# Value passes unit by unit, expert products in strips of 32 columns, and wider spacing of the score groups in an attention and expert kernel

## The chip, the cores and the metric

The kernel runs on one core of one Trainium2 chip. The metric is the device time of one execution in microseconds (us), the median of three runs; lower is better.

## The reference

```python
# q, k, v: (8 batches, 12 heads, 448 tokens, 64)
scores = (1 / sqrt(64)) * q @ k^T;  attn = softmax(scores);  a = attn @ v
x = a.transpose(0, 2, 1, 3).reshape(3584, 768)
h = x @ w_in               # 768 x 2048
g = h * sigmoid(h)
out = g @ w_out            # 2048 x 768, float32
```

## The kernel before

**Units.** Heads go in groups of four, three groups to a batch. A unit is one group of one batch: 448 queries (in batch 0, 224, so that it starts sooner). The 448 keys of a group are laid out as four chunks. The first four groups are "lone": their chunks have 128, 128, 96 and 96 keys. The others go in pairs, ten of them: each has three full chunks and a rest of 64 keys, and the rests of the two groups of a pair stand in one chunk, the "low" group's in partitions 0 to 63 and the "high" group's in 64 to 127.

**TensorE's four shapes.** A matmul may use only part of the array, and then several run at once.

- Scores (`score`, L323): 32 rows by 128 columns, the four heads at once, each over 64 channels in two steps (L327). A pair has three score groups for each unit and one for both rests (`scores_rest`, 32x64, eight matmuls at once for each step).
- Sums (`attend_sums`, L398): 128x32, four heads at once, three steps for a pair (L406).
- Value passes (`attend`, L414): one for each half of the 64 output channels (`part` 1 and 2). For a pair one pass makes both units: three steps of 128x32 for each, in two PSUM banks, then one step of eight 64x32 matmuls for the two rests (L390 through `attend_mm`). That is seven steps, 24 matmuls of 128x32 and 8 of 64x32.
- Experts: full 128x128. `ffn1` (L484) multiplies by `w_in`, six matmuls of 448 columns for each of 16 blocks (L487). `product` (L682) multiplies by `w_out` with a scheme of seven products in the place of eight for two token tiles and two column halves (a "quad", L685), eight matmuls of 384 columns each; the sums that it needs are made on VectorE (`combine_g`, L656). The first four output tiles are made plainly (`plain`, L695, L699). The last two batches' `w_in` products use a scheme of seven too (`pair_product`, L603, L622).

**Other engines.** ScalarE makes the exponentials (L364), tanh (L498) and later silu, VectorE the transposes of Q and K, the reciprocals of the sums, the scaling of the value passes (`norm`, L468, L473) and the gates (L533). GpSimd issues all loads, in the order of `plan_k`, `plan_q` and `plan_v`; SyncE issues the stores.

**The order of the work** is not that of loops. `Order` (L78) is a planner that runs while the kernel is built: each piece of work is an `Op` with an engine, a guessed time and what it depends on; the planner steps a clock, and at each step gives ScalarE and VectorE the ready `Op` that has waited longest (corrected by a bias), and TensorE what the loop at L1443 picks. The code is then emitted in the planned order, and the engines follow it by semaphores. The loop picks a score group if its inputs and buffers are ready and the planned clock has come to `pace["next"]` (or no expert work is ready), and runs ready value work behind it; otherwise ready value work if there is any; otherwise the first ready expert product of the list `moe`. `pace["next"]` goes up by `PACE` for each score group of batches from 2 on. It may lag behind the clock by a credit of 4 us. A change of shape is charged with `SWITCH` (0.094 us, `on_pe`, L106). `Ring`s stand for buffers: two pairs of PSUM banks for scores, four banks ("m") for all other outputs, nine tiles of exponentials, two tiles of V. `SHY` makes VectorE hold back unimportant work if urgent work is about to come.

Of the kernel before, what the change touches and what calls it, by code (L numbers as in the profile page):

```python
# [9 lines left out]
FP16 = mybir.dt.float16  # L10
# [54 lines left out]
class Op:  # L65


    def __init__(self, eng, busy, emit, deps=(), bias=0.0, tail=HOP, then=None):
        self.eng, self.busy, self.emit = eng, busy, emit
        self.deps, self.bias, self.tail, self.then = list(deps), bias, tail, then  # L70
        self.done = None
        self.half = False

    def ready(self):
# [3 lines left out]
class Order:  # L78


    def __init__(self, shy):
        self.now, self.shy = 0.0, shy
        self.free = {"PE": 1.0, "ACT": 2.1, "DVE": 1.2, "POOL": 1.2}
        self.wait = {"ACT": [], "DVE": []}
        self.pool = []
        self.dma_free = 0.0
        self.out = []
        self.mode = None
        self.busy = {e: 0.0 for e in self.free}

# [7 lines left out]
    def start(self, op):  # L98
        self.emit(op.emit)
        self.free[op.eng] = self.now + op.busy  # L100
        self.busy[op.eng] += op.busy
        op.done = self.now + op.busy + op.tail
        if op.then:
            op.then(op.done)

    def on_pe(self, op, mode):  # L106
# [59 lines left out]
def kernel(  # L166
# [28 lines left out]
    NRK, NRQ = 3, 4  # L195
    PACE = 2.6
    LONES = (0, 1, 2, 3)
# [4 lines left out]
    COLD, FIRST = 8.5, 47  # L202
    SHY = 0.5
    TWB, SXB = 4, 4
# [33 lines left out]

    rawk, rawq, KT, QT, VT, E, T, acc, rdn_t, xT, g_t, ost_t = ({} for _ in range(12))
    sT_t, inv_t = {}, {}  # L240
# [23 lines left out]
    def load_v(b, hg0, hg1, x):  # L264
        if b not in VT:
            VT[b] = sb.tile([128, NH, NCH, D], FP16, name=f"V_{b}", tag="V", bufs=2)
        hs = slice(HG * hg0, HG * hg1)
        first, count = X_TOK[form(b, hg0)][x]
        nc.gpsimd.dma_start(  # L269
            out=VT[b][32 * x : 32 * (x + 1), hs, 0:count, :],  # L270
            in_=v[b, hs].rearrange("h (i g) d -> i h g d", g=TPP)[
                :, :, first : first + count, :
            ],
        )
# [107 lines left out]
    def attend_mm(a, n, part, c, h, k0, k1, e, start, stop):  # L382
        b, hg, g0, g1 = units[n]
        nq = 32 * (g1 - g0)
        at = nq * (c % per_burst(n))
        if part == 0:
            w = ones[k0:k1, :]
        else:
            w = VT[b][k0:k1, HG * hg + h, c, part - 1 :: 2]
        nc.tensor.matmul(  # L390
            out=a[32 * h : 32 * (h + 1), 0:nq],
            lhsT=w,
            rhs=e[k0:k1, h, at : at + nq],
            start=start,
            stop=stop,
        )
# [17 lines left out]
    def attend(ns, part):  # L414
        made = []
        lone = len(ns) == 1
        if part == 0 and not lone:
# [66 lines left out]
    def ffn1(b, f, t0, t1):  # L484
        h = ps.tile([128, 512], FP32, name=f"h_{b}_{f}_{t0}", tag="m", bufs=4)
        for cc in range(NDC):
            nc.tensor.matmul(  # L487
                out=h[:, 0 : t1 - t0],
                lhsT=w_in_t[:, cc, 128 * f : 128 * (f + 1)],
                rhs=x3(b, cc)[:, cc % 3, t0:t1],  # L490
                start=(cc == 0),
                stop=(cc == NDC - 1),
            )
        h_t[(b, f, t0)] = h
# [60 lines left out]
    def old_buffer(name, home, cols):  # L555

        if home == "V":
            t = sb.tile([128, NH, NCH, D], FP16, name=name, tag="V", bufs=2)
            t = t.rearrange("p h c d -> p (h c d)")
# [43 lines left out]
    def pair_product(f, m):  # L603
# [17 lines left out]
        for c in range(3):  # L621
            nc.tensor.matmul(  # L622
                out=pp_t[(f, PBANK[m])],
                lhsT=w[:, c, :],
                rhs=a[:, c, :],
                start=(c == 0 and m in (1, 6, 5)),
                stop=(c == 2),
                skip_group_check=True,
            )
# [45 lines left out]
    def product(qd, m):  # L675
# [8 lines left out]
        for f in range(HF):  # L684
            nc.tensor.matmul(  # L685
                out=pr_t[(qd, BANK[m])][:, 0:OH],
                lhsT=w[:, f, :],
                rhs=W_[m][:, f, :],
                start=(f == 0 and BANK[m] == m),
                stop=(f == HF - 1),  # L690
                skip_group_check=True,
            )


    def plain(t, j, f0, f1):  # L695
        if f0 == 0:
            pr_t[("o", t, j)] = ps.tile([128, 512], FP32, name=f"o_{t}_{j}", tag="m", bufs=4)
        for f in range(f0, f1):
            nc.tensor.matmul(  # L699
                out=pr_t[("o", t, j)][:, 0:OH],  # L700
# [228 lines left out]
    def queue_pair():  # L929
        xs = {(r, c): x_op[(PB + r, c, 0)] for r in range(2) for c in range(NDC)}  # L930
        v_ring.take()
        e_ring.take(2)
        od.add(
            Op(
                "ACT",
                2.7,
                first_silu,
                [x for f in range(NFF) for x in g_op[(PB - 1, f)]],
                -5,
            )  # L940
        )
        for m in range(1, 5):
# [8 lines left out]
        for f in range(HF):  # L951
            queue_pair_f(f, xs)

    def queue_pair_f(f, xs):
# [284 lines left out]
    jobs.sort()  # L1239
    qk_seq, av_seq = [], []  # L1240
    for ns in jobs:
# [85 lines left out]
    def av_at():  # L1327
# [3 lines left out]
        if len(ns) == 2 and part == 0:  # L1331
            if any(len(t_op.get(n, ())) < 2 for n in ns):
                return None
# [6 lines left out]
        for n in ns:  # L1340
            if len(exp_op.get(n, ())) < 2 * NCH // per_burst(n):
                return None
            first = 0.0 if n == ns[0] else (NCH - 1) * mm(S)
            for i, x in enumerate(exp_op[n]):
                c = i // 2 * per_burst(n)
                if len(ns) == 2 and c == NCH - 1:
                    c = 2 * (NCH - 1) - (n != ns[0]) * (NCH - 1)
                deps.append((x, first + c * mm(32 * (units[n][3] - units[n][2]))))
            if part:
# [10 lines left out]
    def run_av():  # L1360
# [4 lines left out]
        if part == 0:  # L1365
            m_ring.take()
            mms = 3 if two else 4
        else:
            m_ring.take(len(ns))
            mms = 7 if two else 4  # L1370
        op = Op(
            "PE",
            mms * mm(nq) + 0.013 + (0.03 + SWITCH if two and part else 0.0),
            lambda: attend(ns, part),
            tail=PE_OUT,
        )
        if part == 2:

            def then(at):
                for _ in range(7 if two else NCH // per_burst(ns[0])):  # L1380
                    e_ring.give(at)
                if any(units[n][1] == NG - 1 and units[n][3] == TPP for n in ns):
                    v_ring.give(at)

            op.then = then
# [3 lines left out]
        if two and part:  # L1389
            od.mode = "rest cols"  # L1390
        if part == 0:
# [51 lines left out]
    while True:  # L1443
        plan_turns(qk_seq[0][0][0] + 3 if qk_seq else NU)
        plan_adds()
        plan_pair()
        plan_sums()
        soon = od.step()
        if od.free["PE"] <= od.now:
# [81 lines left out]
```

## Time and profile before

| | |
|---|---|
| median of 3 runs | 396.54 us (396.23 to 396.64) |
| profiled execution | 396.11 us, of which the span is 394.3 us |
| instructions | 9242 |
| granted TensorE clock | 1.0 in every slice |
| VectorE, ScalarE busy | 69%, 64% of the span |
| DMA | 34.43 MB in 35579 packets, mean 87 GB/s |

The span is the time from the first to the last instruction of the program; the rest of the execution lies around it. In rows of the time line a start, a length, the engine, the line, the operation, `out<-in`, the shape of the array (rows*columns), the shape of the moving operand and a count follow one another. Matmuls overlap in the pipeline, so a row's length is longer than the distance to the next start: the distance is what a piece of work costs.

### The profile page before, as it was taken

To read this page: it belongs to the slowest core of one execution; us is meant where nothing else is said; L and a number is where in the kernel's file an instruction comes from. 1 tells how busy PE (TensorE), PEld (TensorE's weight loads), DVE (VectorE), ACT (ScalarE), POOL (GpSimd) and SP (SyncE) were. 2 spreads that over 40 slices of the span, in tenths; PEclk is the share of its full clock that TensorE was granted. 3 is DMA by queue.
4 is the path that set the end of the run, shared out by engine and by line. 5 is a ranking of instruction groups with operands and counts; after the bars stand their busy time and mean duration, and the time that the engine had idled before them with its cause. 6 is when DMAs were issued, how large, how long until landed. Compare 5 with 4: busy or idle time off the path is not lost.

```text
span 394.3 us, 9242 instructions
## 1 busy us (share of the span) xinstructions
PE 387.6 (98%) x3679; PEld 200.0 (51%) x3679; DVE 272.7 (69%) x570; ACT 253.6 (64%) x404; POOL 83.6 (21%) x153
## 2 busy tenths in 40 slices
PE   8999999999999999999999999999999999999995
PEld 7667764443444444554444444444444555555563
DVE  2466676999967588963698576896879945457332
ACT  4988885696871986753974759867685236763221
POOL 7532547215001532330006131600000000000000
PEclk9999999999999999999999999999999999999999
DMA  7999999919033946292016683711100130001343
GB/s 116 204 210 210 162 179 187 154 35 141 13 65 79 148 56 86 50 193 62 2 23 90 116 162 52 98 24 31 51 2 7 33 99 25 2 1 29 95 110 90
DMA packets 35579, 34.43 MB, mean 87 GB/s; under 512 B 11600, under 2 KB 34000, under 8 KB 35536
## 3 DMA queue, kind: packets, MB, share of 16 engines
q0 software_dynamic: 24784, 22.82, 38.7%
q1 hardware_dynamic: 9984, 10.24, 9.6%
q10 hardware_dynamic: 768, 0.79, 0.8%
q8 instruction: 29, 0.48, 0.5%
q14 instruction: 14, 0.11, 0.1%
HBM read 45.61 MB, written 11.01 MB: 144 GB/s over the span
## 4 chain that ended last, share of the span: by engine, by line
PE 91%; DVE 4%; ACT 1%; DMA 1%; issue 1%; ACTq 0%; POOL 0%; DVEq 0%; POOLq 0%
PE p L685 28%; PE h L487 28%; PE s L327 12%; PE a L390 10%; PE f L622 8%; PE o L699 3%; PE a L406 2%; DMA rq<-in_q_dram 1%; DVE tw L598 1%; ACT E L364 1%; PE z L1438 1%; DVE G L533 1%; ACTq L734 0%; DVE S L671 0%; DVE G L671 0%
## 5 line engine op out<-in xcount | busy, mean ns | idle before, releaser
L364 ACT ACTIVATE E<-s 128x896 f16<-128x896 f32 (+1 forms) x172 | 149.9, 915 | 22.6 <-PE s L327 21.2
L487 PE MATMUL h<-xT,w_in_t 128*128 128x448 f16 (+1 forms) x672 | 118.9, 327 | 0.0
L487 PEld LDWEIGHTS <-w_in_t 128*128 128x128 f16 x672 | 61.1, 98 | 54.4 <-issue 18.8
L498 ACT ACTIVATE th<-h 128x448 f16<-128x448 f32 (+1 forms) x112 | 54.3, 495 | 31.6 <-PE h L487 21.5
L533 DVE SCALAR_TENSOR_TENSOR G<-th,h 128x448 f16<-128x448 f16 (+2 forms) x112 | 55.1, 507 | 16.0 <-ACT th L498 14.0
L685 PE MATMUL p<-w_out_t,G 128*128 128x384 f16 x368 | 65.3, 326 | 0.3 <-DVE xT L473 0.2
L685 PEld LDWEIGHTS <-G 128*128 128x128 f16 x472 | 45.3, 98 | 33.4 <-issue 4.0
L269 POOL DMA_DIRECT2D V<-in_v_dram x88 | 48.6, 570 | 57.1 <-PE a L390 43.6
L327 PE MATMUL s<-rq,KT 32*128 32x448 f16 (+4 forms) x864 | 56.7, 340 | 0.6 <-ACT E L364 0.4
L742 ACT COPY ost<-p 128x384 f32<-128x384 f32 x39 | 18.7, 479 | 48.5 <-PE p L685 33.5
L390 PE MATMUL a<-E,V 128*32 128x448 f16 (+3 forms) x864 | 40.6, 335 | 0.0
L473 DVE SCALAR_TENSOR_TENSOR xT<-a,rdn 128x448 f16<-128x448 f32 (+1 forms) x54 | 28.9, 568 | 12.5 <-PE a L390 11.7
L254 POOL DMA_DIRECT2D rq<-in_q_dram x27 | 15.2, 561 | 105.2 <-PE s L327 85.8
L685 PE MATMUL p<-D,S 128*128 128x384 f16 x208 | 37.4, 327 | 0.0
L327 PEld LDWEIGHTS <-KT 32*128 32x128 f16 (+2 forms) x864 | 17.5, 98 | 28.7 <-issue 25.9
L390 PEld LDWEIGHTS <-V 128*32 128x32 f16 (+2 forms) x864 | 18.2, 95 | 22.6 <-issue 15.3
L375 DVE TENSOR_TENSOR T<-T,E 128x1792 f16<-128x1792 f16 x20 | 21.7, 1086 | 11.4 <-ACT E L364 11.4
L685 PEld LDWEIGHTS <-S 128*128 128x128 f16 x208 | 19.4, 98 | 16.2 <-issue 3.1
L375 DVE TENSOR_TENSOR T<-E,E 128x1792 f16<-128x1792 f16 x20 | 21.7, 1083 | 7.8 <-ACT E L364 7.8
L647 ACT ACTIVATE G<-f 128x448 f16<-128x448 f32 x32 | 16.2, 547 | 8.4 <-PE f L622 8.3
L304 DVE STREAM_TRANSPOSE KT<-rk 128x256 f32<-128x256 f32 (+3 forms) x48 | 16.6, 384 | 5.9 <-DMA rk<-in_k_dram 5.8
L314 DVE STREAM_TRANSPOSE rq<-rq 128x448 f32<-128x448 f32 (+1 forms) x27 | 15.3, 570 | 6.0 <-DMA rq<-in_q_dram 5.9
(124 smaller groups left out, 323.6 us busy)
## 6 DMA issues: line engine op xcount, KB each, us to landing
out_dram<-ost SPq DMA_DIRECT2D x208, 48.0 KB, 1.6
rk<-in_k_dram POOLq DMA_DIRECT2D x24, 224.0 KB, 4.9
rq<-in_q_dram POOLq DMA_DIRECT2D x21, 224.0 KB, 5.2
w_in_t<-in_moe_w_in_dram POOLq DMA_DIRECT2D x6, 512.0 KB, 11.6
w_out_t<-in_moe_w_out_dram POOLq DMA_DIRECT2D x4, 768.0 KB, 12.9
V<-in_v_dram POOLq DMA_DIRECT2D x43, 64.0 KB, 3.8
V<-in_v_dram POOLq DMA_DIRECT2D x40, 48.0 KB, 3.6
out_dram<-ost ACTq DMA_DIRECT2D x16, 48.0 KB, 1.8
```

The costliest lines, as they stand in the source:

```text
L269: nc.gpsimd.dma_start(out=VT[b][32 * x : 32 * (x + 1), hs, 0:count, :], in_=v[b, hs].rearrange("h (i g) d -> i h g d", g=TPP)[:, :, first ...
L327: nc.tensor.matmul(out=pS[p0 : p0 + 32 * (x1 - x0), h % 2, at : at + nq], lhsT=KT[(b, hg)][32 * h : 32 * (h + 1), c, x0:x1, :, e], rhs=QT[ ...
L364: nc.scalar.activation(out=E[(n, w)][0:kr, 2 * y : 2 * y + 2, 0:nk], in_=pS_t[(n, w, y)][0:kr, :, 0:nk], func=AF.Exp, scale=attn_scale,)
L375: nc.vector.tensor_tensor(out=T[n], in0=T[n] if step else E[(n, 0)], in1=E[(n, step + 1)], op=ALU.add,)
L390: nc.tensor.matmul(out=a[32 * h : 32 * (h + 1), 0:nq], lhsT=w, rhs=e[k0:k1, h, at : at + nq], start=start, stop=stop,)
L473: nc.vector.scalar_tensor_tensor(out=x3(b, cc)[:, cc % 3, 32 * g0 : 32 * g1], in0=acc[(n, part)][:, 0:nq], scalar=0.5, in1=rdn_t[n].rearra ...
L487: nc.tensor.matmul(out=h[:, 0 : t1 - t0], lhsT=w_in_t[:, cc, 128 * f : 128 * (f + 1)], rhs=x3(b, cc)[:, cc % 3, t0:t1], start=(cc == 0), s ...
L498: nc.scalar.activation(out=th, in_=h_t[(b, f, t0)][:, 0 : t1 - t0], func=AF.Tanh)
L533: nc.vector.scalar_tensor_tensor(out=dst[:, f, at + lo : at + hi], in0=th_t[(b, f, t0)][:, lo - t0 : hi - t0], scalar=1.0, in1=h_t[(b, f, ...
L622: nc.tensor.matmul(out=pp_t[(f, PBANK[m])], lhsT=w[:, c, :], rhs=a[:, c, :], start=(c == 0 and m in (1, 6, 5)), stop=(c == 2), skip_group_ ...
L685: nc.tensor.matmul(out=pr_t[(qd, BANK[m])][:, 0:OH], lhsT=w[:, f, :], rhs=W_[m][:, f, :], start=(f == 0 and BANK[m] == m), stop=(f == HF - 1),
L742: nc.scalar.copy(out=ost(qd, i, j), in_=bank(qd, m))
```

## The change

1. **Value passes unit by unit.** `av_seq` has the sums of a pair as before, and then parts 1 and 2 of each unit by itself, in one PSUM bank: four steps of four 128x32 matmuls. The fourth step takes the shared chunk with all 128 rows; for the other unit's half to add nothing, V holds zeros there. The two V tiles become fixed buffers, and `clear_v` writes these zeros: two memsets at the start, four when batches 0 and 1 are done with their tiles.
2. **Experts in strips.** While attention isn't finished and the four plain tiles are planned, `ffn1`, `product` and the others run each matmul as four of 128x32, one for each 32 output rows, over the same moving operand (`wide`). The planner counts them as the shape of the value passes ("cols"), without a change.
3. **Spacing.** `PACE` goes from 2.6 to 4.0 and the credit from 4 to 8 us. `SHY` goes to 0.
4. The first silu, which loads ScalarE's table, is planned when all value passes and the last `ffn1` have been planned.

```diff
     def on_pe(self, op, mode):
+        if mode == "full" and self.attention:
+            mode, op.strips = "cols", True
         gap = SWITCH if mode != self.mode else 0.0
...
-    PACE = 2.6
+    PACE = 4.0
...
-    SHY = 0.5
+    SHY = 0.0
...
+    VT = [const.tile([128, NH, NCH, D], FP16, name=f"V{i}") for i in range(2)]
+
+    def clear_v(i, hg, low):
+        rows = slice(64, 128) if low else slice(0, 64)
+        nc.vector.memset(VT[i][rows, HG * hg : HG * (hg + 1), NCH - 1], 0.0)
+
+    for hg in (1, 2):
+        clear_v(1, hg, hg == 1)
...
+    def wide(out, lhsT, rhs, **flags):
+        n = 4 if od.strips else 1
+        for j in range(n):
+            at = slice(128 // n * j, 128 // n * (j + 1))
+            nc.tensor.matmul(out=out[at], lhsT=lhsT[:, at], rhs=rhs, **flags)
...
         for n in ns:
             a = ps.tile([128, 512], FP32, name=f"a_{n}_{part}", tag="m", bufs=4)
-            made.append(a)
             acc[(n, part)] = a
-            for c in range(NCH if lone else NCH - 1):
+            for c in range(NCH):
+                e = E[(lead.get(n, n) if c == NCH - 1 else n, c // per_burst(n))]
                 for h in range(HG):
                     attend_mm(
-                        a, n, part, c, h, 0, rows_of(n, c), E[(n, c // per_burst(n))],
-                        c == 0, lone and c == NCH - 1,
-                    )
-        if not lone:
-            for h in range(HG):
-                for i, n in enumerate(ns):
-                    attend_mm(
-                        made[i], n, part, 3, h, 64 * i, 64 * (i + 1), E[(ns[0], 3)],
-                        False, True,
+                        a, n, part, c, h, 0, rows_of(n, c), e, c == 0, c == NCH - 1
                     )
...
-            nc.tensor.matmul(
+            wide(
                 out=h[:, 0 : t1 - t0],
...
-        av_seq += [(ns, part) for part in range(3)]
+        av_seq.append((ns, 0))
+        av_seq += [([n], part) for n in ns for part in (1, 2)]
+        lead[ns[-1]] = ns[0]
...
+        od.attention = bool(qk_seq or av_seq) and len(plain_op) == 4
...
-                pace["next"] = min(max(pace["next"], od.now - 4), od.now) + (
+                pace["next"] = min(max(pace["next"], od.now - 8), od.now) + (
                     PACE if u0[0] > EAGER else 0.0
                 ) * len(qk_seq[0][2]) / 2
```

More of the change, by code (lines that the diff above doesn't have):

```diff
@@ L72, in __init__ @@
         self.half = False
+        self.strips = False
     def ready(self):
@@ L88, in __init__ @@
         self.mode = None
+        self.strips = False
+        self.attention = True
         self.busy = {e: 0.0 for e in self.free}
@@ L414, in attend @@
     def attend(ns, part):
-        made = []
-        lone = len(ns) == 1
-        if part == 0 and not lone:
+        if part == 0 and len(ns) == 2:
             attend_sums(ns)
@@ L952, in queue_pair, with plan_silu @@
             queue_pair_f(f, xs)
+    silu_op = []
+    def plan_silu():
+        if silu_op or av_seq or ffn1_left[PB - 1]:
+            return
+        deps = [x for f in range(NFF) for x in g_op[(PB - 1, f)]]
+        silu_op.append(od.add(Op("ACT", 1.4, first_silu, deps, -5)))
     def queue_pair_f(f, xs):
@@ L1239 @@
     jobs.sort()
-    qk_seq, av_seq = [], []
+    qk_seq, av_seq, lead = [], [], {}
     for ns in jobs:
@@ L1342, in av_at @@
                 return None
[L1343 removed]
             for i, x in enumerate(exp_op[n]):
                 c = i // 2 * per_burst(n)
[L1346 to L1348 removed]
+                deps.append((x, c * mm(32 * (units[n][3] - units[n][2]))))
             if part:
@@ L1368, in run_av @@
         else:
-            m_ring.take(len(ns))
-            mms = 7 if two else 4
+            m_ring.take()
+            mms = 4
         op = Op(
             "PE",
-            mms * mm(nq) + 0.013 + (0.03 + SWITCH if two and part else 0.0),
+            mms * mm(nq) + 0.013,
             lambda: attend(ns, part),
@@ L1379, in then @@
             def then(at):
-                for _ in range(7 if two else NCH // per_burst(ns[0])):
+                n = ns[0]
+                for _ in range(NCH // per_burst(n) - (lead.get(n + 1) == n)):
                     e_ring.give(at)
@@ L1383, in then @@
                     v_ring.give(at)
+                    i = units[ns[-1]][0]
+                    for hg in range(NG if i == 0 else 1 if i == 1 else 0):
+                        low = i == 0 and hg != 1
+                        od.add(
+                            Op("DVE", 0.2, lambda hg=hg, low=low: clear_v(i, hg, low), [op], 5)
+                        )
             op.then = then
```

36 lines of the change are left out of this document (13 added, 23 removed).

## The prediction

> **What bounds the kernel now.** I read the engine sums first, then TensorE's waits, then TensorE's time line.
>
> ```profile
> PE 387.6 (98%) x3679; PEld 200.0 (51%) x3679; DVE 272.7 (69%) x570; ACT 253.6 (64%) x404; POOL 83.6 (21%) x153
> ```
>
> ```profile
> PE a L390 <- issue: 0.5, 1, 0.5
> ```
>
> TensorE is busy for 98% of the span, and once it has begun its longest wait is this one of half a microsecond. So the time is the sum of TensorE's own work, and the only thing to gain is what TensorE spends that isn't streaming. In the two stretches below the columns are: length, busy time and instructions of matmuls, weight loads, DVE, ACT and POOL, then clock, DMA share and GB/s:
>
> ```profile
> 14.40:27.40 13.00, 13.00 (x294) 8.34 (x293) 7.85 (x23) 11.83 (x14) 6.31 (x10) 1.00 1.13 210
> 75.60:305.30 229.70, 229.58 (x2126) 102.89 (x2123) 179.15 (x358) 161.18 (x242) 46.60 (x86) 1.00 0.41 69
> ```
>
> The second stretch is what the change works on: from the end of the four plain output tiles (75.6) to the last value pass (305.4). The groups of that stretch, by shape:
>
> ```profile
> L487 PE MATMUL h<-xT,w_in_t 128*128 128x448 f16 x480 | 98.9, 353 | 0.0
> L685 PE MATMUL p<-w_out_t,G 128*128 128x384 f16 x216 | 39.1, 326 | 0.1
> L327 PE MATMUL s<-rq,KT 32*128 32x448 f16 x408 | 29.3, 360 | 0.0
> ...
> L685 PE MATMUL p<-D,S 128*128 128x384 f16 x112 | 20.4, 327 | 0.0
> L685 PE MATMUL p<-D,G 128*128 128x384 f16 x56 | 10.3, 327 | 0.0
> L390 PE MATMUL a<-E,V 64*32 64x448 f16 x144 | 6.9, 360 | 0.0
> L327 PE MATMUL s<-rq,KT 32*64 32x448 f16 x144 | 5.4, 368 | 0.0
> ```
>
> 480+216+112+56 and 24 more of the products on X (26 with two last plain ones) are 890 full 128x128 matmuls. 408/8 + 144/16 = 60 score groups, 144/8 = 18 value passes of a pair. Each change of the array's shape costs, and the time line prices it (first column is the start):
>
> ```profile
> 173.78 2.43 PE L487 MATMUL h<-xT,w_in_t 128*128 128x448 f16 x12
> 176.05 2.76 PE L685 MATMUL p<-w_out_t,G 128*128 128x384 f16 x16
> 178.75 1.63 PE L390 MATMUL a<-E,V 128*32 128x448 f16 x32
> 180.31 0.99 PE L685 MATMUL p<-D,G 128*128 128x384 f16 x5
> ```
>
> ```profile
> 199.86 0.36 PE L406 MATMUL a<-E,both 128*32 128x448 f16 x4
> 200.16 2.44 PE L487 MATMUL h<-xT,w_in_t 128*128 128x448 f16 x12
> 202.53 0.57 PE L327 MATMUL s<-rq,KT 32*128 32x448 f16 x8
> 203.04 1.31 PE L487 MATMUL h<-xT,w_in_t 128*128 128x448 f16 x6
> ```
>
> Starts tell the price, not durations. Full to full, 12 matmuls take 176.05-173.78 = 2.27, so one is 0.189 (0.162 at 384 columns, by the ratio). 16 of those are 2.60, and 178.75-176.05 is 2.70: full to 128x32 costs **0.10**. The sums' last group of four at once took 0.30: 0.189 and **0.11** back to full. 202.53-200.16 = 2.37: full to scores **0.10**; the score group's 0.51 is two steps (0.378) and **0.13** back. The value pass took 1.56: seven steps (1.324), and **0.24** for going to 64x32 inside it and back to full behind it.
>
> **The change, part by part.** *Value passes.* A pair's pass now has seven steps and 0.24; two single passes have eight (1.514), all of one shape. 18 x (1.56-1.514) = -0.8.
>
> *Experts as strips.* Four 128x32 matmuls have the value passes' shape, so going between experts, sums and value passes no longer drains. By the time line nine of these blocks are entered from an expert (eight single value passes and the sums at 297.61) and all nine sums are left for one: 9 x 0.105 + 9 x 0.11 = -1.9 (the exits of the value passes are in the term above). Does a strip group stream as fast as one full matmul? Rows of batch 0, four at once over only 224 columns:
>
> ```profile
> 31.64 0.95 PE L390 MATMUL a<-E,V 128*32 128x224 f16 x32
> 32.52 0.65 PE L487 MATMUL h<-xT,w_in_t 128*128 128x224 f16 x5
> ```
>
> ```profile
> 16.06 0.57 PE L390 MATMUL a<-E,V 128*32 128x224 f16 x16
> 16.56 0.57 PE L327 MATMUL s<-rq,KT 32*128 32x224 f16 x8
> ```
>
> Eight groups in 0.88, less 0.10 for the exit, are 0.097 each; half of 0.189 is 0.095. Four weight loads and four matmuls fit into 0.097, and a strip group has 0.162 or 0.189 for them: I cost it at nothing. Bounds: below, nothing excludes a few ns but nothing shows them; above, see the rivals. The new price is at the scores: 16.56-16.06 = 0.50, less four steps of 0.096, is 0.12 from 128x32 to scores, against 0.10 from full. 60 x 0.01 to 0.02: +0.6 (to 1.2; I take the lower, the starts being rounded).
>
> The Trainium skill speaks against strips: "TensorEngine Tiling (Array Packing)", Restrictions, says that column tiling turns Fast Weight Load off, and "TensorE: Matmul & The Clock Gate", The mechanism, that weight loads hide beside running matmuls only where the row group differs, which strips of 128 rows don't. By that rule each group would show its loads; the rows of batch 0 just quoted disagree.
>
> *Single passes in the plain stretch.* The first pair's two passes (69 to 74) lie before strips begin and may become four: at most two more pairs of drains, +0.4; nothing if they run back to back. I take +0.2.
>
> *Memsets, the shy rule, the table load.* Two memsets before the first transposes and four later ones are DVE work beside a TensorE that doesn't wait for DVE; DVE is at 69%. The later ones wait for a batch's last value pass, with adds and gates behind them on DVE, but they are planned once that pass is issued and the next reader is a value pass two batches on; if DVE stood at them, an m bank would come free late, and there are four. One m bank at a time instead of two makes a value pass start earlier, which moves work but removes none. Nothing. The table load still comes after the last value pass and lies on ACT (64%).
>
> *Wider spacing.* It removes no work; it moves the end of attention. Now:
>
> ```profile
> 67.41 0.58 PE L327 MATMUL s<-rq,KT 32*128 32x448 f16 x8
> ```
>
> ```profile
> 294.65 0.60 PE L327 MATMUL s<-rq,KT 32*64 32x448 f16 x16
> 295.18 2.44 PE L487 MATMUL h<-xT,w_in_t 128*128 128x448 f16 x12
> 297.61 0.56 PE L406 MATMUL a<-T,half 128*32 128x448 f16 x8
> ...
> 300.84 1.63 PE L390 MATMUL a<-E,V 128*32 128x448 f16 x32
> 302.40 1.47 PE L685 MATMUL p<-w_out_t,G 128*128 128x384 f16 x8
> 303.81 1.64 PE L390 MATMUL a<-E,V 128*32 128x448 f16 x32
> 305.37 0.82 PE L685 MATMUL p<-D,S 128*128 128x384 f16 x4
> ```
>
> ```profile
> 317.40 0.73 PE L622 MATMUL f<-xT,w_in_t 128*128 128x448 f16 x3
> ...
> 319.32 2.76 PE L685 MATMUL p<-w_out_t,G 128*128 128x384 f16 x16
> ```
>
> 63 score groups (nine pairs of seven) carry the spacing, and 227.2 / 62 = 3.7 us lie between them on average; 2.6 didn't bind. With 4.0 and a credit of 8 the last one may come at 67.4 - 8 + 4 x 62 = 307.4, some 13 later (sooner where no expert is ready). Behind it the chain to the last value pass is 2.96 to the sums (two exponentials lie between), 3.23 to the first value pass (the reciprocal chain on DVE), and four single passes of 4 x 0.189: 9.2, of which attention's own work is 0.53 + 0.57 + 3.03 = 4.1. So **5.1 us** of experts must be left for it. Now 10.7 less 0.53, 0.57, two passes of 1.56 and some drains, 6.1, lie inside that chain, 12.0 between 305.37 and 317.40, where the pair's products begin, and at least 16 x 0.162 = 2.6 are mixed into these: 20.7. Take away 13 to 14 for the later end and 1.5 to 2 for the gain: 5 to 6 are left. It covers, barely. I add +0.4 of idle time, nearer the covered end (0) than the uncovered one (5). The loads go along: POOL's queue waits for score groups anyway,
>
> ```profile
> POOL rq L254 <- PE s L327: 85.8, 8, 25.8
> ```
>
> so Q, K and V of the next units are issued later, into DMA engines that are busy for 0.41, and nothing else stands in that queue by then. The output stores are in SP's and move with their products.
>
> **Sum:** -0.8 -1.9 +0.6 +0.2 +0.4 = **-1.5** against the profiled execution's 396.11. That lies 0.43 under the median of the runs, so the median should go from 396.54 to about **395.0**.
>
> **Rivals.** *(1) The junction runs dry.* Attention's end becomes the chain, and TensorE idles before the pair's products. For: the margin above is under 1 us out of 20.7, and dependences inside the last quads may make the left-over experts unready. Against: scores run early whenever no expert is ready. Idle of 2 to 5 us instead of 0.4: 396.6 to 399.6. It cancels the gain from 1.9 us on.
>
> *(2) Instruction supply, on the slow side.*
>
> ```profile
> q8 instruction: 29, 0.48, 0.5%
> ```
>
> 7358 TensorE instructions (two rows of 3679) came in these 29 packets of the instruction queue, 254 each. In batch 0 TensorE once stopped inside a group, for nothing that the profile shows; I read it as a wait for instructions:
>
> ```profile
> 28.43 0.28 PE L390 MATMUL a<-E,ones 96*32 96x224 f16 x3 [0.49 <-issue]
> ```
>
> That was behind a stretch with 587 instructions in 13 us (45 per us) at a DMA share of 1.13. The second stretch has 4249, 18.5 per us at 0.41; with strips it gets 4249 + 6 x 890 = 9589, 42 per us, 38 packets. One stop of 0.49 in the 2.3 packets of the first stretch would, for 38, be 8 us; scaled by the DMA share 3: 398 to 403. It turns slower from five stops on. Against: at 0.41 a packet rarely meets full queues, and I count none in the sum. "Runtime: NRT & Kernel Launch", Instruction fetch mechanics, of the Trainium skill, calls the cost of crossing from one such block to the next mostly hidden; with the reading above the trace agrees but for that one stop of 0.49.
>
> *(3) The shape isn't what drains.* If strips of 128 columns still drain against value passes (the cost lying in the change of operands, not of shape), only the value passes' inner 64x32 step goes: 396.0 to 396.6, no change. Against: the eight groups from 31.64 on, each with other weights and other data, are 0.097 apart without a drain.
>
> *(4) Weight loads show.* Weight loads of this shape last
>
> ```profile
> L390 PEld LDWEIGHTS <-V 128*32 128x32 f16 x432 | 9.9, 96 | 11.5 <-issue 5.3 <-DMA V<-in_v_dram 0.4
> ```
>
> If each strip group paid one such time, 890 x 0.096 = 85: 481. Against: the 224-column groups, 0.097 apart with everything in them. It is what the Trainium skill's rule above would make of this kernel.
>
> **How the numbers follow.** Forecast, 393.4 to 395.7: 0.58. Better still (idle gone, no price at the scores, earlier passes): 0.05, not under 393. Junction dry: 0.16, of which half stays within the bound. Instruction supply: 0.14, slower. Shape: 0.05, no change. Loads: 0.02. A measurement of this kernel can tell about 0.2% from no change, 0.8 us. Faster: 0.58 + 0.05 = 0.63. Same: half of 0.16 and 0.05, 0.13. Slower: the other half, 0.14 and 0.02, 0.24. The range reaches from the better case through the dry junction and the milder part of the supply rival: 393.0 to 400.0.
>
> **What would show it.** The time line after should show no extra 0.10 between strips and value passes, 1.51 for a unit pair's two passes, strip groups at 0.162 and 0.189, and 0.12 ahead of each score group. A TensorE gap near 318 is the junction; gaps marked "issue" inside strip groups, many with a busy DMA, are the supply. I am wrong if strip groups stream slower than 0.19, or if attention ends well past 320.

## The result, and the profile after

The changed kernel takes 395.24 us (median, 394.45 to 395.75) against 395.91 for the kernel before on the same chip: ratio 0.998, 95% interval [0.9971, 0.9989]. A second set of runs gave 394.79 us and 0.9977 [0.9967, 0.9986]. It is faster by 0.2%. The time itself is close to the forecast (395.0), but the step to it is 0.67 us (1.1 in the second set) where 1.5 was forecast: the forecast started from 396.54, the median of three executions, and the median of eleven is 0.63 lower. The gain is so small that the terms behind it are the more interesting question. I compare spans below, since the part outside the span turned out to vary: the median span of the kernel before is 394.2 us, that of the changed one 392.9 to 393.0. Four executions in all the runs below, with a granted clock of 0.95 to 0.96 and times of 410 to 412 us, are left out of medians and ratios.

The page of the changed kernel, engine sums and instruction queue:

```profile
PE 384.7 (98%) x6607; PEld 213.9 (54%) x6607; DVE 272.9 (70%) x576; ACT 253.9 (65%) x404; POOL 83.6 (21%) x153
...
q8 instruction: 51, 0.84, 0.9%
```

TensorE has 80% more instructions and yet 2.9 us less of busy time; the instruction queue brings 51 packets in the place of 29. The waits of TensorE (us in total, times, longest):

```profile
PE z L1452 <- DVE zeros L230: 1.0, 1, 1.0
PE s L349 <- DVE rq L330: 0.9, 1, 0.9
PE f L337 <- ACT G L658: 0.6, 1, 0.6
PE s L349 <- ACT E L386: 0.4, 1, 0.4
```

Nothing is marked "issue". All but the third come in the first eight microseconds (at 0.99, 6.10 and 7.68); that of 0.9 for `rq` is also in a second profile of the kernel before. The third, at 325.70, is new: it is the junction of rival 1, 0.63 us deep. The two stretches of the prediction, the second one up to the new end of attention:

```profile
14.40:27.40 13.00, 13.00 (x292) 8.35 (x288) 8.04 (x23) 11.86 (x14) 5.79 (x9) 1.00 1.13 210
75.60:317.10 241.50, 241.20 (x5136) 125.61 (x5128) 185.60 (x373) 163.24 (x247) 45.21 (x83) 1.00 0.41 72
```

5136 + 5128 instructions in 241.5 us are 42 per us, as forecast, at the forecast DMA share of 0.41. TensorE's time line, a long row of strips and then the end of attention:

```profile
192.13 3.59 PE L337 MATMUL h<-xT,w_in_t 128*32 128x448 f16 x72
195.65 0.60 PE L349 MATMUL s<-rq,KT 32*64 32x448 f16 x16
...
307.68 0.61 PE L349 MATMUL s<-rq,KT 32*64 32x448 f16 x16
308.22 1.49 PE L337 MATMUL p<-D,S 128*32 128x384 f16 x32
309.53 1.47 PE L337 MATMUL p<-w_out_t,G 128*32 128x384 f16 x32
310.83 0.55 PE L428 MATMUL a<-T,half 128*32 128x448 f16 x8
311.21 0.36 PE L428 MATMUL a<-E,both 128*32 128x448 f16 x4
311.40 2.77 PE L337 MATMUL p<-w_out_t,G 128*32 128x384 f16 x64
314.00 3.20 PE L412 MATMUL a<-E,V 128*32 128x448 f16 x64
317.13 1.47 PE L337 MATMUL p<-D,G 128*128 128x384 f16 x8
318.44 2.65 PE L337 MATMUL f<-xT,w_in_t 128*128 128x448 f16 x12
...
325.70 0.73 PE L337 MATMUL f<-xT,w_in_t 128*128 128x448 f16 x3 [0.63 <-ACT G L658]
```

Read the starts again. 195.65-192.13 = 3.52 for 72 strips, 18 groups: less 0.11 for the change to scores, 0.189 each, what a full matmul took. 310.83-309.53 = 1.30 is eight groups of 0.162 with nothing added for going to the sums; 311.40-311.21 = 0.19 leaves the sums for nothing; 314.00-311.40 = 2.60 is 16 groups, with nothing for going to the value passes. 317.13-314.00 = 3.13 is 16 steps of 0.189 and 0.10 back to the full array. So the prices of the prediction stand in the trace one by one. The last score group starts at 307.68 (forecast 307.4) and the pair's products at 318.44, one later than before.

To add up all of it I took, in the second trace of each kernel (`before_again`, `after_again`), every distance between two matmul starts, took off the streaming time (0.189 us for 448 columns, in proportion for others) and grouped what is left by the shapes on both sides:

| us over the span | before | after | difference | the prediction's term |
|---|---|---|---|---|
| streaming (20 passes with one step more) | 353.02 | 356.81 | +3.79 | |
| changes to and from 64x32 | 4.59 | 0 | -4.59 | with the row above -0.80: "-0.8" |
| between 128x32 and full, 25 changes, then 8 | 2.54 | 0.80 | -1.74 | "-1.9" |
| into score groups | 8.53 | 9.38 | +0.85 | "+0.6" |
| out of score groups | 10.30 | 10.15 | -0.15 | |
| stops, behind the first 10 us | 1.87 | 2.82 | +0.95 | "+0.4" |
| the rest | 7.57 | 7.30 | -0.27 | |
| sum | | | -1.16 | -1.5 |

The last matmul ends 1.17 us earlier (388.57 against 389.74). Of the stops, 0.79 is the junction.

### The profile page after: what moved, and what is told of

The parts are those of the page before. It is cut to its first block, busy times and chain, and to the rows that moved or that the text cites. A ratio compares the mean times of both kernels' runs of the same rounds, so it can differ in the third digit from the quotient of the medians.

```text
span 392.5 us, 15118 instructions
## 1 busy us (share of the span) xinstructions
PE 384.7 (98%) x6607; PEld 213.9 (54%) x6607; DVE 272.9 (70%) x576; ACT 253.9 (65%) x404; POOL 83.6 (21%) x153
## 4 chain that ended last, share of the span: by engine, by line
PE 95%; ACT 2%; DMA 1%; DVE 1%; issue 0%; ACTq 0%; DVEq 0%; POOLq 0%
PE p L337 30%; PE h L337 29%; PE s L349 12%; PE a L412 11%; PE f L337 8%; PE o L337 3%; PE a L428 2%; DMA rk<-in_k_dram 1%; PE z L1452 1%; ACT E L386 1%; ACTq L745 0%; DVE p L757 0%; ACT ost L753 0%; DVE KT L320 0%; DVE ost L762 0%
## 5 line engine op out<-in xcount | busy, mean ns | idle before, releaser
L337 PE MATMUL h<-xT,w_in_t 128*32 128x448 f16 (+1 forms) x2112 | 118.0, 345 | 0.0
L337 PEld LDWEIGHTS <-w_in_t 128*32 128x32 f16 (+1 forms) x2184 | 73.1, 97 | 56.6 <-issue 15.7
L337 PEld LDWEIGHTS <-G 128*32 128x32 f16 (+1 forms) x1520 | 54.2, 97 | 37.4 <-issue 7.6
L337 PE MATMUL p<-w_out_t,G 128*32 128x384 f16 (+1 forms) x1160 | 65.6, 326 | 0.3
L412 PE MATMUL a<-E,V 128*32 128x448 f16 (+2 forms) x864 | 41.9, 333 | 0.0
L337 PE MATMUL p<-D,S 128*32 128x384 f16 (+1 forms) x640 | 37.0, 326 | 0.0
L485 DVE SCALAR_TENSOR_TENSOR xT<-a,rdn 128x448 f16<-128x448 f32 (+1 forms) x54 | 29.8, 568 | 8.6 <-PE a L412 7.2
L412 PEld LDWEIGHTS <-V 128*32 128x32 f16 (+1 forms) x864 | 21.0, 97 | 17.8 <-issue 6.2
L337 PEld LDWEIGHTS <-S 128*32 128x32 f16 (+1 forms) x640 | 22.3, 97 | 12.2 <-issue 1.1
L658 ACT ACTIVATE G<-f 128x448 f16<-128x448 f32 x32 | 16.3, 547 | 9.0 <-PE f L337 8.9
```

The source lines that it names most:

```text
L337: nc.tensor.matmul(out=out[at], lhsT=lhsT[:, at], rhs=rhs, **flags)
L412: nc.tensor.matmul(out=a[32 * h : 32 * (h + 1), 0:nq], lhsT=w, rhs=e[k0:k1, h, at : at + nq], start=start, stop=stop,)
L485: nc.vector.scalar_tensor_tensor(out=x3(b, cc)[:, cc % 3, 32 * g0 : 32 * g1], in0=acc[(n, part)][:, 0:nq], scalar=0.5, in1=rdn_t[n].rearra ...
L658: nc.scalar.activation(out=G[:, f, S * r : S * (r + 1)], in_=pp_t[(f % HF, x)], func=AF.Silu, scale=2.0,)
```

## The experiments

Each kernel ran beside the kernel before. `before_again` and `after_again` are the two kernels once more.

> The kernel before against itself, for its spread and for the time that lies outside its span (1.81 us in the profile of before, 3.25 in that of after: the span fell by 1.8, the profiled execution by 0.36 only). Theory (the shape changes explain it, and something at the program's end gives part back): ratio 1.000, spans of 394.0 to 394.5 in every run, 1.8 outside. Rival (the gain of the span was luck of one profile): spans spread as widely as after's, 392.5 to 393.9.

395.95 us, ratio 1.0004 [0.9995, 1.0013]; spans of 393.8 to 394.9, wider than expected, and 1.73 to 1.84 us outside. Its trace has no stop marked "issue": the 0.49 us at 28.43 that the prediction read as a wait for instructions is marked in some executions only.

> The changed kernel once more. Theory: spans of 392.5 to 393.9 and a median 0.5 to 1.0 under before; part of its executions have 2.2 to 3.3 us outside the span, as three of eleven had, the others 1.8. Rival (instruction supply): spans differ from run to run because TensorE waits inside strip groups; the profile shows such waits marked issue, of 0.3 to 0.7 each.

394.79 us, 0.9977, as above; spans of 392.7 to 393.4.

**One part alone, or all but one.** `strips_only` is the kernel before with the strips:

```diff
+        if mode == "full" and self.attention:
+            mode, op.strips = "cols", True
...
+        od.attention = bool(qk_seq or av_seq) and len(plain_op) == 4
```

> Before, with the experts in strips and nothing else: the pair's value passes keep their 64x32 step, the spacing stays 2.6. Theory: nine entries from experts and nine exits of the sums go, 18 x 0.105 = -1.9, the price ahead of 60 score groups stays, +0.6: span -1.3, to about 393.0. Rival (instruction supply): 12688 instead of 7360 TensorE rows cost stops of 0.5; from three stops on the span is no shorter than before.

395.07 us, 0.9978 [0.9968, 0.9988], median span 393.25: 0.85 less than the kernel before beside it (394.1), not 1.3. This is most of the gain: the changed kernel, on the same chip, has the ratio 0.9977 and a span of 392.9, so value passes and spacing together add 0.35 us of span to what strips do alone.

`passes_only` is the changed kernel without strips and with the old spacing:

```diff
-    PACE = 4.0
+    PACE = 2.6
...
-    SHY = 0.0
+    SHY = 0.5
...
-        od.attention = bool(qk_seq or av_seq) and len(plain_op) == 4
+        od.attention = False
...
-                pace["next"] = min(max(pace["next"], od.now - 8), od.now) + (
+                pace["next"] = min(max(pace["next"], od.now - 4), od.now) + (
```

> After, with full matmuls for the experts and the old spacing, credit and shy rule: only the value passes unit by unit. By its order of work there are 22 ways from sums and passes into experts (before: 25, of which some 13 come out of the 64x32 step) and 9 from experts into them (before 13). Theory: -0.8 for the passes, about +1.0 for ten more exits at 0.105, -0.4 for four entries less: -0.2, no change. Rival (the passes are what gains, by one bank instead of two): -1 or more.

397.48 us, 1.0042 [1.0028, 1.0055], median span 395.5: slower, where no change was expected. The term itself is there (no 64x32 stop is left, -0.8 with the added steps), but the changes between 128x32 and full rise from 2.54 to 3.32 us, and two stops of 0.93 and 0.73 come at 301.35 and 305.65.

`old_spacing` is the same with the strips left in (only `PACE`, `SHY` and the credit go back).

> After, with the spacing at 2.6, the credit at 4 and the shy rule at 0.5 again: strips and unit passes alone. Its order of work has as many visits to scores (86) and as few changes of shape as after's. Theory (the spacing only moves attention's end): span like after's, 392.9, give or take 0.3; if the junction's one wait in after's profile (0.63 us, for a silu on ACT, at 325.7) is the price of the late end, up to 0.6 less. Rival (the wider spacing is what gains): slower than after by 1 us or more, as passes alone were 1.4 slower than before with new waits at 300 and 304.

397.03 us, 1.003 [1.0019, 1.0041], median span 395.1. So what the spacing is worth in the changed kernel is 395.1 - 392.9 = 2.2 us, nearly twice the gain of the whole change. (`PACE`, credit and `SHY` always moved together; which of them it is was not separated.) The time line of TensorE in `old_spacing` shows where:

```profile
297.14 3.36 PE L412 MATMUL a<-E,V 128*32 128x448 f16 x64
301.66 1.29 PE L337 MATMUL h<-xT,w_in_t 128*128 128x448 f16 x6 [1.17 <-DVE xT L485]
...
304.82 1.46 PE L337 MATMUL p<-w_out_t,G 128*128 128x384 f16 x8 [0.57 <-ACT 1_8_7757 L750]
```

and that of VectorE at the same place:

```profile
298.12 0.62 DVE L485 SCALAR_TENSOR_TENSOR xT<-a,rdn 128x448 f16<-128x448 f32 x1
...
299.25 1.82 DVE L609 TENSOR_TENSOR tw<-w_in_t 128x1536 f16<-128x1536 f16 x2
300.99 1.15 DVE L485 SCALAR_TENSOR_TENSOR xT<-a,rdn 128x448 f16<-128x448 f32 x2
```

Four single value parts run back to back, each into an m bank, and there are four. The next expert needs a bank, and a bank comes free when VectorE has scaled it (`xT`, L485): the expert starts at 301.66, when the second scaling ends. But two sums of weights for the last batches (`tw`, L609), 1.82 us that nobody is waiting for, stand ahead of the second scaling. In the changed kernel the same four parts (314.00 above) are followed by a product (317.13) that goes on in a bank it has, so TensorE doesn't stop there.

`old_norms_first` tests this reading: `old_spacing` with one rule more in the planner.

```diff
             m, f0 = pair_todo[0]
+            if f0 == 4 and (qk_seq or av_seq):
+                return
...
-                    [pair_w[(k, f0)] for k in {2: (1,), 4: (2,)}.get(m, ())],
+                    [pair_w[(k, f0)] for k in {2: (1,), 4: (2,)}.get(m, ())] + norm_op[-4:] * (f0 == 4),
```

> This is the changed kernel with the old spacing, and with one rule more: VectorE's weighting of the next expert's second half is not put ahead of the last norms of attention. The old spacing alone gave a span of 395.1 with a wait of 1.2 us for xT and one of 0.6 us for a value bank. Theory (the weighting of 1.82 us stands ahead of the norms on VectorE and holds the next expert's input): the wait of 1.2 us goes, span 393.6 to 394.2. Rival (the four banks that the value parts fill are the cause, whatever VectorE does first): a wait of 0.8 us or more stays, span 394.7 to 395.3.

395.33 us, 0.9981 [0.9971, 0.999], median span 393.55. The wait for `xT` is gone, the one behind it is not:

```profile
297.60 3.36 PE L412 MATMUL a<-E,V 128*32 128x448 f16 x64
300.89 1.31 PE L337 MATMUL h<-xT,w_in_t 128*128 128x448 f16 x6
...
304.07 1.46 PE L337 MATMUL p<-w_out_t,G 128*128 128x384 f16 x8 [0.56 <-ACT 1_8_7757 L750]
```

VectorE's order accounts for 395.1 - 393.55 = 1.55 of the 2.2 us, and the rival (banks alone) falls. The size is uncertain by some tenths: the spans of this kernel reach from 392.7 to 394.4, and its profiled execution (394.1) has another wait, of 1.03 us at 242.22 for VectorE's gates, which is 0.3 in `old_spacing`. What stays at 304.07 is a product that waits for ScalarE to copy another one out of its bank (L750).

`no_strips` is the changed kernel with `od.attention = False`: passes and spacing without strips.

> This is the changed kernel with the experts' later groups as one 128x128 matmul per block again; unit value passes and wide spacing stay. Theory (the strips take away the stops between column and full groups, about 0.105 us each, 25 of them before against 8 after): those stops come back, about 18 of 0.105 us = 1.9 us, or up to 3 us since the 64x32 stops before scores also return; less 0.01 us on each of 60 score entries (0.0958 from full, 0.106 from strips) = -0.6. Span 394.2 to 396.0 beside 392.9 for the change. Rival (the strips are no more than a cover for the pace of the scores, and the wide spacing alone gives the gain): span 392.5 to 393.3.

397.41 us, ratio 1.0044 [1.0032, 1.0056], median span 395.3: 2.4 more than with strips. The cause shows in the same block of both kernels; here `no_strips`,

```profile
172.65 2.77 PE L337 MATMUL p<-w_out_t,G 128*128 128x384 f16 x16
175.35 0.94 PE L412 MATMUL a<-E,V 128*32 128x448 f16 x16
```

and here `after_again`:

```profile
172.31 2.78 PE L337 MATMUL p<-w_out_t,G 128*32 128x384 f16 x64
174.92 0.93 PE L412 MATMUL a<-E,V 128*32 128x448 f16 x16
```

The block takes 2.70 us from start to start against 2.61: the 0.09 is the change of shape, and there are 37 of these in `no_strips` against 8 (3.70 us against 0.80). At 2.9 us these changes are more than the loss. At the old spacing the strips were worth only 0.85 us beside pairs and 0.4 beside unit passes, though they take away as many changes there (25 to 8, 32 to 9). Stops are larger beside them (2.45 us against 1.87, 4.73 against 3.00), but part of that lies ahead of the first strip (at 28.45 in `strips_only`, 0.66 us against 0.28 in `before_again`; at 22.84 and 28.39 in `old_spacing`), and there is one trace of each. Why strips bring less at the old spacing stays open.

`strips_spaced` is `strips_only` with `PACE` 4.0, the credit of 8 and `SHY` 0.

> This is the kernel before with strips and with the wide spacing, but with value passes for pairs of head groups. strips_only had a median span of 393.25. Theory (wide spacing only takes away a jam that four single value parts in a row make at the end of attention, and pairs do not make it): no gain from the spacing here, span 393.0 to 393.7. Rival (wide spacing gains by itself, by fewer or cheaper score groups in the strips): span 391.0 to 392.2.

399.78 us, 1.0105 [1.0092, 1.0119], median span 397.5. Both expectations failed: with pairs of value passes the wide spacing neither gains nor is neutral, it costs 4.2 us. The first rows of its waits:

```profile
PE p L330 <- DVE S L686: 2.3, 4, 0.8
PE f L330 <- DVE sx L595: 1.4, 1, 1.4
```

Experts catch up with the sums that VectorE makes for them (four times, at 104 to 108 and 158 to 162), and the junction waits for sums of inputs; all stops grow from 2.45 to 6.87 us, which is about the whole loss. At the junction VectorE has the order seen above: two `tw` (321.46, 1.82 us) stand ahead of the last two scalings (323.20), and the sum that TensorE waits for begins at 325.13. That this order is the cause here was not tested, and why VectorE is late at 104 to 108 and 158 to 162 with pairs and not with single passes I have not separated.

| passes by unit | strips | wide spacing | run | ratio to before | median span |
|---|---|---|---|---|---|
| | | | before_again | 1.0004 | 394.2 |
| | x | | strips_only | 0.9978 | 393.25 |
| x | | | passes_only | 1.0042 | 395.5 |
| x | x | | old_spacing | 1.003 | 395.1 |
| x | | x | no_strips | 1.0044 | 395.3 |
| | x | x | strips_spaced | 1.0105 | 397.5 |
| x | x | x | after_again | 0.9977 | 392.9 |

Wide spacing alone was not run.

**Instruction supply.** `strips_from_start` uses strips in batch 0 and in the plain tiles too:

```diff
-        od.attention = bool(qk_seq or av_seq) and len(plain_op) == 4
+        od.attention = bool(qk_seq or av_seq)
```

> After, with strips also for batch 0's expert input passes (192 matmuls of 224 columns become 768) and the plain tiles, so in the stretch from 30 to 75 us where the DMA engines are busiest; 14750 instead of 13216 TensorE rows. A strip group of 224 columns asks for eight instructions in 0.095 us, 84 per us, twice the rate of the strips so far. Instruction supply as a limit: 254 instructions a packet last 3 us there, the packets took about 1 us each and came up to 5 us late in that stretch: stops marked issue of 1 to 3 us for each of some five packets, 3 to 10 us slower than after. Theory (supply is hidden): within 0.5 of after.

409.02 us, 1.0335 [1.0313, 1.0357], span 406.7 in the profile: 13.8 us more than the changed kernel, where 3 to 10 was expected if instructions limit. The first waits of TensorE, and its time line behind them:

```profile
PE h L337 <- issue: 8.0, 4, 2.3
PE a L412 <- issue: 1.5, 1, 1.5
PE p L337 <- DVE S L682: 1.4, 2, 0.8
PE s L349 <- issue: 1.1, 1, 1.1
```

```profile
32.23 0.55 PE L412 MATMUL a<-E,V 128*32 128x224 f16 x13
34.29 0.66 PE L412 MATMUL a<-E,V 96*32 96x224 f16 x19 [1.51 <-issue]
...
40.21 1.81 PE L337 MATMUL h<-xT,w_in_t 128*32 128x224 f16 x67 [2.15 <-issue]
```

TensorE stops inside a group, where no data can be awaited: 13 matmuls of the group are done, then nothing for 1.51 us, then the other three. Two things in the trace tie these stops to the instruction queue. The six that are marked "issue" come behind matmuls 476, 603, 731, 859, 1115 and 1243 of the program, so 127 or 128 apart or twice that, and 128 matmuls with their weight loads are 256 instructions, what a packet holds (below). And each ends 1.3 to 1.5 us after a packet of that queue has landed (at 34.29 after a packet that landed at 33.03, at 40.21 after one of 38.87). The stop of the kernel before at 28.43 lies behind the same 476th matmul, 1.47 us after its packet. A strip of 224 columns starts every 0.024 us (0.097/4), 82 instructions per us with its weight load, where the DMA engines are full of the first loads (a share of 1.16 from 30 to 45, 1.05 from 45 to 60). That is the rival "instruction supply", with a price above its own range: 10.6 of the 13.8 us are marked "issue", and from 45 to 60 the granted clock is 0.89 besides, against 1.00 in the changed kernel. In the change it doesn't act, since strips begin behind this stretch (75.18), with half the rate and a third of the load.

"Runtime: NRT & Kernel Launch", Instruction fetch mechanics, of the Trainium skill, calls the cost of crossing from one block of instructions to the next mostly hidden. With 51 packets and no stop marked "issue" the changed kernel agrees; `strips_from_start`, with stops of 1.1 to 2.3 us, does not.

**The end of the program.** The profiled execution of the changed kernel took 395.75 us, 3.25 more than its span, where the kernel before has at most 1.85 in 70 executions. Six of the 22 executions have such long ends (2.09 to 3.25). Behind the last instruction, from 392.5 to 397, its DMA view has

```profile
q8 instruction: 1, 0.02, 1.7%
```

and that of the kernel before, behind 394.3, has

```profile
DMA packets 0, 0.00 MB, mean 0 GB/s; under 512 B 0, under 2 KB 0, under 8 KB 0
```

51 packets for 13,216 TensorE instructions (counted in the program) and 29 for 7,360 are about 256 to a packet. Theory: TensorE's program ends near the edge of a packet, so that the last packet is fetched when the program is nearly over, and some executions wait for it. In the trace of `after_again`, with 1.74 us outside the span, the last packet comes at 386.16, seven microseconds ahead of the end; in the execution above it comes at 394.77. `after_shifted` moves the edge by 120 instructions: 20 of the 47 warm-up matmuls on zeros become four strips each.

```diff
+        for i in range(n):
+            parts = 4 if n == FIRST and i >= n - 20 else 1
+            for j in range(parts):
+                at = slice(128 // parts * j, 128 // parts * (j + 1))
```

> After, with 20 of the 47 zero matmuls that warm TensorE up at the start cut into strips of 32 columns: the same time, but 120 more TensorE rows (13336), so that the last block of 256 instructions ends elsewhere. In after (13216 rows) the profile with 3.25 us outside its span shows an instruction packet 2 us behind the span's end, that with 1.74 outside shows the same packet 7 us ahead of it. Theory (the block's end falls on the program's end by chance): no execution with over 2 us outside, span 392.9, median about 394.7. Rival (the long ends belong to strips as such): a third of the executions still has 2.1 to 3.3 outside.

394.37 us (394.1 to 394.49), 0.9957 [0.9945, 0.997]; 1.73 to 1.80 us outside the span in all five, and 1.76 to 1.79 in the five of `best` (below), which has the same 13,336 instructions. `before_edge` does the opposite to the kernel before: 224 more, 7,584, which lies 22 x 256 below 13,216.

> Before, with 37 of the warm-up zero matmuls in strips of 32 columns and one in two of 64: 224 more TensorE rows, 7584, which stand to the blocks of 256 as after's 13216 do (160 over a whole number). Theory: some of its executions have 2.1 to 3.3 us outside the span, where before had 1.73 to 1.85 in all of 24; spans as before, 394.1. Rival (strips as such, or the longer program): all executions at 1.7 to 1.9.

395.81 us, 0.9998 [0.9989, 1.0007], but with ends of 2.06, 2.49 and 2.99 us in three executions, which the kernel before has in none. `strips_spaced`, again with 13,216, has one of 3.53, and its profile too shows a packet behind the last instruction (at 398.67, where the span ends at 397.5). All this fits the theory without proving it: where exactly the edge lies was not counted, and why the packet is late in some executions only is open. The price in the median is small, as most executions don't pay. It is not all that varies: `passes_only` and `old_spacing` have 1.9 us outside the span throughout, `no_strips` 2.1, `strips_spaced` 2.1 to 2.3 in its other four, for reasons that I did not find.

**Together.** `best` is `after_shifted` with the rule of `old_norms_first`.

> This is the changed kernel with 20 of the 47 warm-up matmuls cut into four strips (TensorE then has 13336 instructions, so the end of the program is not at a multiple of 256), and with the rule that the weighting does not go ahead of the last norms. The first alone gave a median of 394.37 and a span of 392.6. Theory (in the wide spacing VectorE's order at the end of attention holds nobody): as that, span 392.3 to 392.9, median 394.1 to 394.6. Rival (the junction's wait of 0.6 us is for VectorE too): span 391.8 to 392.2.

393.18 us (393.08 to 393.39), 0.9929 [0.9917, 0.9941], median span 391.4: the theory that VectorE's order holds nobody fell, and the gain is larger than the rival's range. The rule alone is worth 392.6 - 391.4 = 1.2 us here. All waits of TensorE that are left:

```profile
PE z L1457 <- DVE zeros L230: 1.0, 1, 1.0
PE s L349 <- ACT E L386: 0.4, 1, 0.4
```

The junction is gone. VectorE in `after_shifted`,

```profile
315.14 0.62 DVE L485 SCALAR_TENSOR_TENSOR xT<-a,rdn 128x448 f16<-128x448 f32 x1 [0.42 <-PE a L412]
315.68 1.82 DVE L609 TENSOR_TENSOR tw<-w_in_t 128x1536 f16<-128x1536 f16 x2
317.42 1.68 DVE L485 SCALAR_TENSOR_TENSOR xT<-a,rdn 128x448 f16<-128x448 f32 x3
319.01 0.85 DVE L591 TENSOR_TENSOR V<-xT,xT 128x1344 f16<-128x1344 f16 x1
...
324.20 1.20 DVE L649 TENSOR_TENSOR f<-f,p 128x448 f32<-128x448 f32 x2 [0.29 <-PE f L337]
```

and in `best`:

```profile
314.71 1.38 DVE L485 SCALAR_TENSOR_TENSOR xT<-a,rdn 128x448 f16<-128x448 f32 x2 [0.42 <-PE a L412]
316.01 0.85 DVE L591 TENSOR_TENSOR V<-xT,xT 128x1344 f16<-128x1344 f16 x1
316.77 1.15 DVE L485 SCALAR_TENSOR_TENSOR xT<-a,rdn 128x448 f16<-128x448 f32 x2
...
322.42 1.20 DVE L649 TENSOR_TENSOR f<-f,p 128x448 f32<-128x448 f32 x2 [0.32 <-ACT G L658]
```

The wait that the profile puts down to ScalarE's G (L658, the silu that reads a bank of `f` and so frees it) began ten microseconds ahead of it on VectorE: the same 1.82 us of `tw` stand between the scalings, the sums of inputs come behind these (L591), and then the additions on `f` (L649) that silu waits for. With `tw` out of the way the sums begin at 316.01 and not at 319.01, and the additions at 322.42 and not at 324.20.

## Why the prediction was right, point by point

- **Value passes**, "-0.8": -0.80. The passes were 20, with the first pair's in them, so "+0.2" for these was not there.
- **Experts as strips**, "-1.9" and "I cost it at nothing" for the streaming: -1.74, 17 changes fewer, and strips stream as full matmuls do. "TensorEngine Tiling (Array Packing)", Restrictions, of the Trainium skill, says that column tiling turns Fast Weight Load off; if it does here, it costs nothing at 0.189 us per group of four.
- **Price ahead of scores**, "+0.6 (to 1.2)": +0.85. By the same distances an entry is 0.096 us from the full array and 0.106 from strips.
- **The junction**, "+0.4": 0.63 by the profile's row, 0.79 by the distance of the starts. The estimate of the end (307.4; it was 307.68) and of the chain behind it (9.2; 317.13 - 307.68 = 9.45) held, and it "covers, barely" was fair. But the wait isn't where I looked for it, before the pair's products, but inside them, seven microseconds later.
- **The memsets, the shy rule, the table load**, nothing: no new wait names them.
- **What failed** is the step "It removes no work; it moves the end of attention". As an entry in the balance of the finished kernel that is true. As the worth of the edit it is wrong: without it the same kernel is 2.2 us slower, slower than the kernel before. I priced each edit against the trace of before and added up, which assumes that the planner's order has no stop in it with any part missing. Four value parts in a row on four banks make one, and the spacing happens to put a product behind them that needs no bank. That I counted "one m bank at a time instead of two" as "Nothing" has the same fault.
- **Rival 2** was real, but in a stretch that the change leaves alone; the reading of the row at 28.43 is borne out by `strips_from_start`. **Rival 1** took place, at 0.63 to 0.79 us in the place of 2 to 5. **Rivals 3 and 4** fell with the rows from 307.68 on.

That the time came out at 395.24 beside a forecast of 395.0 is partly luck. The sum said -1.5; taken off the 395.91 that the kernel before has in eleven executions it gives 394.4. The span fell by 1.2, so the sum was about right and somewhat too large: the "+0.2" that wasn't there was outweighed by scores and stops, 0.8 more than their "+0.6" and "+0.4". The median moved 0.67 us in the first set, less than the span, because of the long ends; my working had set the outside of the span as the same.

## What to carry to other kernels

If two pieces of work need one array shape, running a full matmul as four column strips is free while a group streams 0.16 us or more and instructions come in time; look at the rate of instructions beside the load of the DMA before using it on short groups. A sum of terms tells what the finished kernel will take, not what an edit is worth. With a planned order every subset with unit passes or wide spacing that ran, short of the whole, was slower than the kernel before (1.0030 to 1.0105), and the whole is faster (0.9977); but strips alone reach 0.9978. So test the parts together, with one left out, and alone: here one part brings most of the gain, and the other two add 0.35 us of span to it. When a wait appears behind a burst of one engine, look at the order on the engine that frees its buffers: here 1.82 us of work that nobody needed yet cost 1.2 to 1.55 (medians of five to twelve executions).

## What the runs showed of the hardware that I had not expected

- With strips of 224 columns (82 TensorE instructions per us), most of them under a DMA share of 1.05 to 1.16, TensorE stood still for instructions for 1.1 to 2.3 us at a time, 10.6 us in all by the profile: at places that are 127 or 128 matmuls apart or twice that, and each time until 1.3 to 1.5 us after an instruction packet had landed.
- With 13,216 or 7,584 TensorE instructions, which are 22 packets of 256 apart, nine of 32 executions ended 0.3 to 1.5 us later (the changed kernel and `before_edge`); with 7,360 or 13,336, none of 80 did (the kernel before, `after_shifted` and `best`). That is not all that decides it: `passes_only` and `no_strips`, also with 7,360, have 1.9 to 2.2 us outside throughout where these have 1.7 to 1.85.
